# Tiles 5 and 6 of q and k loaded four tokens to a partition, W_in in six pieces, and a new order for all engines

## The chip, the core and the metric

The kernel runs on one core of a Trainium2 chip. The time is device time in microseconds (us) of one execution; a kernel's time is the median of several. Matrix products run on TensorE (PE, with its weight loads as PEld), elementwise work on VectorE (DVE) and ScalarE (ACT). GpSimd (POOL) issues most loads and stores, SyncE (SP) the transposing DMAs. Each engine works through its own instructions in program order and waits for the others by semaphores.

## The reference

```python
scores = scale * q @ k.T + bias          # per batch (4) and head (8); 768 tokens, head dimension 64
keep = is_global | is_local              # first 8 keys, and the 96 latest up to the token itself
a = softmax(where(keep, scores, -1e9))
x = (a @ v).transpose(0, 2, 1, 3).reshape(3072, 512)
h = x @ w_in                             # 512 -> 2048
out = (h - tanh(h)) @ w_out              # 2048 -> 512
```

The bias is ALiBi: minus a slope per head times the distance (96 for a far global key). All inputs and the output are float32.

## The kernel before

The 3072 tokens are 24 tiles of 128. They are worked in an order of "turns" u = 0 to 23: the first tile of each of the four batches (turns 0 to 3), then the other tiles, five per batch. "Tile 5" in what follows is turn 5. Below, a dot and a number after a letter names one piece of work; these are the words of the string `ORDER`.

- **Loads.** `lq.u`, `lk.u`, `lv.u` load q, k, v of a tile; `in.j` a piece of W_in, `out.j` a quarter of W_out. For turns 0 to 2 (`u < HW`) q and k come as float32 on ACT's and SP's queues and are cast by `cq.u` and `ck.u` (a trailing `/a` or `/d` says whether ACT or DVE does it). All other loads are POOL's and cast to bfloat16 on the way. For `u < ROWS` `load_rows` puts four tokens of a head into one partition, so that each piece read is 4 x 64 floats (1 KB); from `ROWS` on, and for v, `load_natural` puts one token into one partition, in pieces of 64 floats (256 B).
- **Transposes.** `T.u` turns q and k so that the head dimension lies on the partitions. Up to turn 6 (`u < PE_T`) PE does it. In natural form it is 8 matmuls of 128 columns against `ident` (L313). In the four-token form it is, for turns 3 and up, 16 matmuls with 64-column weights against the permuted identity `turn` (L322), and for turns 0 to 2 it is 8 with 128 columns (L318). `Te.u.1` (k) and `Te.u.0` (q) copy the result from PSUM to `qk`, in the four-token form with a permutation. From turn 7 on, SP issues DMA transposes (L334), from `kq` to `qk`.
- **Attention.** `S` scores (L353; from turn 11 on three blocks at a time), `E` exp on ACT, `M` times the mask table on DVE, `AV` (L379), `R` reciprocal and scaling on DVE. `X.u` and `Xe.u` transpose the result into `xT` (by PE up to turn 7, later by SP's DMAs). `bm.m` and `em.m` build the three mask tables; `K` and `V` copy the global keys and values.
- **MLP.** Tiles are taken in groups: turns 0 and 1 alone, then pairs, then fours. `m1.g.f` is h for 512 output columns of group g (L421): 16 matmuls of 128 columns for a single tile, 8 of 256 for a pair, 4 of 512 for a four. `th` is tanh on ACT (L431), `g` the difference on DVE (L437). `m2.u.0.a` (L446) is a quarter of the sum for the output of tile u: 4 matmuls of 512 columns. `ev` copies it out of PSUM, `st` stores it.
- **Pieces of W_in.** `in_end = [2, 4, 8, 12, 16]`: `in.0` and `in.1` hold two blocks of 128 columns each (512 KB of float32), `in.2` to `in.4` four each (1 MB). `m1.0.0` and `m1.1.0` need `in.0` and `in.1`; `m1.2.0` needs `in.0`, `m1.2.2` needs `in.1`; `m1.0.4`, `m1.1.4`, `m1.2.4` and `m1.2.6` need blocks 4 to 7.
- **Order.** `ORDER` is one list of all pieces of work; each engine takes those that are its own, in that order. `zero:b` is a matmul on zeros whose result nobody uses; it keeps PE at work. `HOMES` gives the buffers and PSUM banks. In the trace of this kernel POOL issues a load only once the load eight places before it has landed, as soon as that many are under way.

What a tile's transpose in PE is, in the code:

```python
if u >= ROWS:
    for p in range(NP):
        nc.tensor.transpose(t[:, p * P : (p + 1) * P], s[:, j, p * P : (p + 1) * P], ident)
...
for hh in range(2):
    c = (hh * R4 + r) * Dh
    nc.tensor.matmul(o[hh * Dh : (hh + 1) * Dh], s[:, j, c : c + Dh], turn, start=True, stop=True)
```

Of the kernel before, what the change touches and what calls it, by code (L numbers as in the profile page):

```python
# [27 lines left out]
Te.6.1/d Te.6.0/a g.2.14 X.4 m2.2.0.1 Xe.4/a lq.9 m2.0.0.2 lv.7 S.6 m2.2.0.2 E.6.1 K.6 m2.1.0.2 E.6.0 M.6.1 m2.3.0.1
M.6.0 m2.2.0.3 T.7 AV.6 ev.2.0/a X.5 R.6 m2.0.0.3 Xe.5/a T.8 m2.3.0.2 V.6 ev.0.0/a T.10 m1.3.12 m1.3.0 th.3.12 T.9
m2.1.0.3 g.3.12 th.3.0 m1.3.8 g.3.0 ev.1.0/a S.7 st.1.0 th.3.8 lq.18 X.6 E.7.1 K.7 m2.3.0.3 g.3.8 lv.12 Xe.6/d m1.3.10  # L30
E.7.0 ev.3.0/d lq.14 m1.3.2 M.7.1 th.3.10 lv.9 m1.3.4 M.7.0 th.3.2 lv.10 g.3.10 S.8 th.3.4 g.3.2 m1.3.6 lq.12 E.8.1
g.3.4 m1.3.14 lk.11 th.3.6 M.8.1 AV.7 lq.11 E.8.0 g.3.6 m2.4.0.0 lk.13 R.7 th.3.14 m2.4.0.1 lk.12 M.8.0 S.9 V.7 lk.14
m2.4.0.2 g.3.14 E.9.0 st.0.0 K.9 X.7 m2.4.0.3 E.9.1 M.9.0 lv.11 S.10 Xe.7/d T.11 lq.13 ev.4.0/a M.9.1 AV.8 E.10.0
m1.4.8 K.10 R.8 T.12 E.10.1 m1.4.10 M.10.0 m2.5.0.0 th.4.8 M.10.1 Xe.8 th.4.10 AV.9 g.4.8 m1.4.2 T.14 V.9 g.4.10
m1.4.6 th.4.2 R.9 m1.4.0 lq.23 th.4.6 g.4.2 Xe.9 AV.10 th.4.0 g.4.6 m2.5.0.1 lk.16 T.13 R.10 m2.5.0.2 g.4.0 Xe.10
m1.4.4 V.10 S.11 th.4.4 lq.22 m2.5.0.3 g.4.4 E.11.1 K.12 m2.6.0.0 K.11 ev.5.0/d E.11.0 m1.4.14 M.11.1 st.5.0 E.12.0
st.2.0 M.11.0 m1.4.12 lv.13 th.4.14 M.12.0 AV.11 lq.15 th.4.12 m2.7.0.0 g.4.14 lk.15 g.4.12 m2.6.0.1 R.11 lk.18
m2.7.0.1 V.11 Xe.11 lq.16 S.12 lv.18 m2.6.0.2 E.13.0 m2.7.0.2 lv.19 E.13.1 M.13.0 m1.5.8 T.15 E.12.1 M.13.1 m1.5.2
th.5.8 M.12.1 m2.7.0.3 T.18 th.5.2 g.5.8 m1.5.4 ev.7.0/a g.5.2 T.16 AV.12 th.5.4 m1.5.0 R.12 m1.5.12 th.5.0 V.12 Xe.12
g.5.4 m1.5.10 th.5.12 lk.19 g.5.0 AV.13 g.5.12 th.5.10 lv.14 m2.6.0.3 R.13 st.4.0 m1.6.2 ev.6.0/a lv.15 g.5.10 Xe.13  # L40
m1.5.6 th.6.2 lk.21 m1.6.12 g.6.2 th.5.6 lq.17 S.13 g.5.6 th.6.12 st.6.0 m1.6.4 g.6.12 lk.17 E.14.1 K.15 K.14 m1.5.14
lq.19 E.15.0 M.14.1 m2.8.0.0 lv.16 th.5.14 M.15.0 m2.8.0.1 E.14.0 g.5.14 m2.8.0.2 th.6.4 M.14.0 m1.6.6 g.6.4 m2.8.0.3
th.6.6 AV.14 g.6.6 ev.8.0/a m1.6.0 T.17 R.14 m1.6.10 th.6.0 V.14 Xe.14 S.14 g.6.0 th.6.10 T.19 m2.10.0.0 g.6.10 E.15.1
K.16 m2.9.0.0 lq.20 E.16.1 M.15.1 m2.10.0.1 st.3.0 E.16.0 M.16.1 lv.17 m2.9.0.1 M.16.0 AV.15 lk.22 m1.6.8 R.15 m1.6.14
th.6.8 V.15 Xe.15 m2.9.0.2 g.6.8 th.6.14 AV.16 g.6.14 m2.9.0.3 V.16 R.16 m2.10.0.2 ev.9.0/a Xe.16 S.15 st.9.0 lq.21
m2.10.0.3 T.22 E.17.0 K.17 m2.11.0.0 ev.10.0/d E.17.1 m2.11.0.1 M.17.0 E.18.0 M.17.1 m1.7.6 M.18.0 S.16 th.7.6
m2.11.0.2 g.7.6 E.18.1 K.19 T.21 m1.7.10 E.19.0 M.18.1 m2.11.0.3 th.7.10 M.19.0 m1.7.1 ev.11.0/a g.7.10 m1.7.2 st.11.0
th.7.1 st.8.0 m1.7.12 g.7.1 th.7.2 lk.20 m1.7.15 g.7.2 th.7.12 st.10.0 m1.7.13 g.7.12 lv.20 th.7.15 m1.7.0 g.7.15
lv.21 th.7.13 AV.17 g.7.13 lv.23 th.7.0 m1.7.3 R.17 E.19.1 lk.23 m1.7.11 V.17 Xe.17 th.7.3 M.19.1 AV.18 th.7.11 g.7.0
m1.7.7 T.20 R.18 m1.7.4 th.7.7 g.7.11 Xe.18 m1.7.9 th.7.4 g.7.7 m1.7.5 th.7.9 g.7.4 m1.7.8 g.7.9 th.7.5 T.23 m1.7.14  # L50
g.7.3 th.7.8 g.7.5 AV.19 th.7.14 m2.13.0.0 g.7.8 V.19 m2.13.0.1 R.19 m2.13.0.2 g.7.14 Xe.19 S.17 m2.12.0.0 E.21.0 K.21
K.20 m2.13.0.3 E.20.0 M.21.0 m2.12.0.1 ev.13.0/d E.20.1 m2.12.0.2 M.20.0 st.13.0 lv.22 M.20.1 S.18 m1.8.2 E.22.1 K.22
# [537 lines left out]
```

## Time and profile before

| | |
|---|---|
| median of 3 runs | 213.57 us (213.45 to 213.74) |
| the profiled execution: time | 213.46 us |
| the profiled execution: span of its instructions | 211.2 us |
| granted TensorE clock | 1.00 in every window of the trace |
| busy share: PE, PEld, DVE, ACT, POOL | 97%, 58%, 63%, 57%, 36% |
| last matmul ends | 208.07 us after the start of the span |

All later times are us from the start of the span. The time of an execution is 2.26 us more than its span; a change of the span is taken to be a change of the time. The views used are the page's sums, the waits by engine (who waited for whom), the chain of work that ended last, the timelines by engine (start, duration, engine, line, operation, destination and source, count, and in brackets the idle time before it and what ended it), and for a DMA its time from issue to landing.

When the loads that POOL issues first landed, from these answers:

| load | lk.3 | lq.3 | lv.1 | lv.0 | lv.2 | in.1 | in.0 | lv.3 | in.2 | lk.5 | in.3 | lk.4 | lq.4 | lq.5 | in.4 | lq.7 | out.0 |
|---|---|---|---|---|---|---|---|---|---|---|---|---|---|---|---|---|---|
| landed | 6.60 | 9.21 | 10.42 | 11.26 | 12.09 | 13.41 | 14.79 | 15.63 | 18.66 | 19.50 | 22.05 | 22.72 | 23.40 | 24.26 | 26.89 | 27.63 | 30.18 |

### The profile page before, as it was taken

Reading aid. Unit: us, or ns where it says so; the run is one execution under the profiler, and the core shown is the slowest. Engines: PE = TensorE matmul, PEld = TensorE weight load, DVE = VectorE, ACT = ScalarE, POOL = GpSimd, SP = SyncE. Lnnn points to the kernel's source line nnn. Section 1 sums busy time; section 2 is a strip of 40 time slices with the busy share of each in tenths; the row PEclk is TensorE's granted clock in tenths of the full one; section 3 lists DMA queues with packets and bytes.
Section 4 is the critical chain, followed back from the end, with each engine's and each line's share of the span. In section 5 each row is a group of like instructions: output and inputs, shape, how many; then the busy total and the mean of one; then the engine's idle time right before and its main releaser. Section 6 shows DMA issues by size and latency. Waiting matters only on the chain.

```text
span 211.2 us, 4631 instructions
## 1 busy us (share of the span) xinstructions
PE 204.8 (97%) x1867; PEld 122.8 (58%) x1867; DVE 132.8 (63%) x269; ACT 120.1 (57%) x177; POOL 77.0 (36%) x101
## 2 busy tenths in 40 slices
...
DMA packets 100885, 27.55 MB, mean 130 GB/s; under 512 B 91841, under 2 KB 99265, under 8 KB 100865
## 3 DMA queue, kind: packets, MB, share of 16 engines
...
q1 hardware_dynamic: 28048, 8.13, 22.4%
...
q8 instruction: 14, 0.23, 0.4%
q14 instruction: 7, 0.05, 0.1%
...
## 4 chain that ended last, share of the span: by engine, by line
PE 90%; DMA 5%; POOL 3%; issue 0%; ACT 0%; POOLq 0%
PE ps L446 40%; PE ps L421 39%; PE ps L353 5%; DMA w_in_bf<-in_moe_w_in_dram 5%; PE ps L379 5%; POOL vb L298 2%; POOL kq L295 1%; POOL w_in_bf L301 1%; PE ps L399 0%; PE ps L313 0%; PE ps L322 0%; POOL rel L236 0%; ACT ot L230 0%; POOLq L236 0%; POOLq L571 0%
## 5 line engine op out<-in xcount | busy, mean ns | idle before, releaser
L421 PE MATMUL ps<-xT,w_in_bf 128*128 128x256 bf16 (+2 forms) x640 | 90.6, 294 | 1.1 <-DMA w_in_bf<-in_moe_w_in_dram 1.1
L446 PE MATMUL ps<-w_out_bf,g 128*128 128x512 bf16 (+2 forms) x400 | 90.2, 371 | 0.0
L437 DVE TENSOR_TENSOR g<-ps,th 128x512 bf16<-128x512 f32 x96 | 65.0, 687 | 37.8 <-ACT th L431 36.5
L431 ACT ACTIVATE th<-ps 128x512 f32<-128x512 f32 x96 | 57.3, 598 | 50.5 <-PE ps L421 49.9
L421 PEld LDWEIGHTS <-w_in_bf 128*128 128x128 bf16 x640 | 56.2, 98 | 28.8 <-DMA w_in_bf<-in_moe_w_in_dram 1.5
L446 PEld LDWEIGHTS <-g 128*128 128x128 bf16 x400 | 37.0, 98 | 39.0
L360 ACT ACTIVATE pr<-ps 128x1024 bf16<-128x1024 f32 x44 | 42.9, 1025 | 12.7 <-PE ps L353 12.0
L455 POOL DMA_DIRECT2D out_dram<-ot x21 | 11.9, 571 | 93.9 <-ACT ot L230 76.5
L364 DVE TENSOR_TENSOR pr<-pr,mk 128x1024 bf16<-128x1024 bf16 x44 | 29.5, 686 | 7.8 <-ACT pr L360 7.5
L298 POOL DMA_DIRECT2D kq<-in_q_dram x19 | 17.2, 907 | 17.5 <-DMA qk<-kq 14.7
L230 ACT COPY ot<-ps 128x512 f32<-128x512 f32 (+2 forms) x20 | 11.3, 564 | 20.7 <-PE ps L446 17.9
L298 POOL DMA_DIRECT2D vb<-in_v_dram x24 | 21.8, 919 | 2.3 <-DMA w_in_bf<-in_moe_w_in_dram 1.7
L298 POOL DMA_DIRECT2D kq<-in_k_dram x19 | 17.3, 923 | 11.3 <-DMA qk<-kq 6.0
L388 DVE TENSOR_TENSOR x<-ps,rden 128x512 bf16<-128x512 f32 x24 | 16.6, 691 | 0.8
L379 PEld LDWEIGHTS <-pr 128*128 128x128 bf16 x352 | 13.5, 97 | 4.3 <-DVE pr L364 0.7
L379 PE MATMUL ps<-vb,pr 128*128 128x65 bf16 x352 | 14.7, 193 | 0.5 <-DVE pr L364 0.5
L353 PEld LDWEIGHTS <-qk 64*128 64x128 bf16 x352 | 10.1, 94 | 5.7 <-issue 4.4
L353 PE MATMUL ps<-qk 64*128 64x128 bf16 x192 | 9.5, 218 | 0.1
L353 PE MATMUL ps<-qk,qk 64*128 64x128 bf16 x160 | 7.8, 217 | 0.0
L387 DVE RECIPROCAL rden<-ps 128x8 f32<-128x8 f32 x24 | 4.8, 199 | 4.1 <-PE ps L379 3.9
L232 DVE COPY qk<-qk 128x32 bf16<-128x32 bf16 x16 | 3.5, 254 | 6.0 <-PE ps L353 6.0
L232 DVE COPY vb<-vb 8x512 bf16<-8x512 bf16 x16 | 6.0, 374 | 1.5 <-PE ps L379 1.5
...
## 6 DMA issues: line engine op xcount, KB each, us to landing
...
```

The source lines that it names most:

```text
L230: nc.scalar.copy(out=out, in_=in_)
L298: eng(e).dma_start(out=dst, in_=rows_of(src, u).rearrange("h p d -> p h d"))
L353: nc.tensor.matmul(bank(("s", u, o), hh)[:, p * P : (p + 1) * P], buf(("qk", back[u] if o else u))[r, 1, p, :], buf(("qk", u))[r, 0, p, :] ...
L360: nc.scalar.activation(d, banks(("s", u, o), 0, 1), AF.Exp, bias=0.0, scale=scale)
L364: nc.vector.tensor_tensor(out=t, in0=t, in1=mk[:, mask_of(u, o)], op=ALU.mult)
L379: nc.tensor.matmul(t[:, h // (H // 2), h % (H // 2), :], buf(("p", u, o))[:, slot(h), :], buf(("v", back[u] if o else u))[:, h, 0 : Dh + 1 ...
L388: nc.vector.tensor_tensor(out=buf(("x", u)).rearrange("q (a h) d -> q a h d", a=2), in0=t[:, :, :, 0:Dh], in1=rden.to_broadcast([P, 2, H / ...
L421: nc.tensor.matmul(t[:, (f - f0) * n : (f - f0 + 1) * n], w_in_bf[j][:, c, fo : fo + P], x[:, c, 0:n], start=(c == 0), stop=(c == CD - 1),)
L431: nc.scalar.activation(h_view(buf(("th", g, f0)), g, m), h_view(bank(("h", g, f0)), g, m), AF.Tanh, bias=0.0, scale=1.0)
L437: nc.vector.tensor_tensor(out=buf(("g", g))[:, f0 : f0 + m, 0:n], in0=h_view(bank(("h", g, f0)), g, m), in1=h_view(buf(("th", g, f0)), g, ...
L446: nc.tensor.matmul(bank(part)[:, 0 : c1 - c0], buf(("g", g))[:, f, t * P : (t + 1) * P], w_out_bf[f // FJ][:, f % FJ, c0:c1], start=(f == ...
L455: eng(e).dma_start(out=out[turn_of[u] * P : (turn_of[u] + 1) * P, c0:c1], in_=buf(("ot", u))[:, c0:c1])
```

## The change

`ROWS` goes from 5 to 7: q and k of turns 5 and 6 come four tokens to a partition, and their `T` and `Te` take the form that goes with it. The third piece of W_in (blocks 4 to 7) becomes two of 512 KB, so that blocks 8 to 11 are now `in.4` and 12 to 15 `in.5`. `ORDER` and `HOMES` are written anew from end to end; below is the new order up to the scores of tile 7, and the old one up to the same place. The work behind it is the same in kind and number, in another order. The loop in `m1` only spells its steps another way. Zero matmuls go from 13 to 11.

```diff
-    ROWS = 5
+    ROWS = 7
...
-    in_end = [2, 4, 8, 12, 16]
+    in_end = [2, 4, 6, 8, 12, 16]
...
-        for f in range(0, CF, m):
+        for f, m in [(f, m) for f in range(0, CF, m)]:
...
-lq.1 lk.1 zero rel ones.0 zero:7 dist lk.3 lq.0 lk.0 zero:7 zero:7 turn lq.2 lk.2 lq.3 slopes zero:7 table zero:7 lv.1
-first bm.1 ident ones.1 lv.0 bm.0 em.1 lv.2 cq.1/d zero:7 ck.1/d em.0 zero:7 in.1 T.1 in.0 cq.0/a zero:7 ck.0/d lv.3
-zero:7 Te.1.1/d Te.1.0/a zero:3 T.0 in.2 S.1 Te.0.1/a Te.0.0/d zero:6 E.1.0 cq.2/d S.0 zero:7 ck.2/d zero:7 lk.5 E.0.0
-M.1.0 T.2 T.3 Te.2.1/d Te.2.0/a in.3 AV.1 M.0.0 Te.3.1/a S.2 lk.4 Te.3.0/a R.1 AV.0 E.2.0 S.3 lq.4 R.0 bm.2 E.3.0 X.1
-M.2.0 lq.5 Xe.1/d em.2 AV.2 X.0 M.3.0 in.4 m1.1.0 Xe.0/a R.2 lq.7 AV.3 th.1.0 R.3 X.2 m1.0.0 Xe.2/a g.1.0 X.3 th.0.0
-Xe.3/d out.0 m1.0.4 g.0.0 lv.5 m1.2.0 th.0.4 m1.2.4 g.0.4 th.2.0 m1.2.2 g.2.0 th.2.4 lv.4 m1.2.6 g.2.4 th.2.2 out.1
-m1.1.4 g.2.2 th.2.6 lv.6 g.2.6 T.4 th.1.4 m1.1.8 lq.6 Te.4.0/d Te.4.1/a g.1.4 m1.0.8 th.1.8 g.1.8 S.4 th.0.8 lk.8
-m1.2.8 E.4.1 K.4 g.0.8 lk.6 m1.2.12 th.2.8 M.4.1 T.5 E.4.0 g.2.8 m1.1.12 Te.5.1/d Te.5.0/a m1.0.12 M.4.0 out.2 th.2.12
...
+lq.1 lk.1 zero rel ones.0 zero:7 dist lk.3 lq.0 lk.0 zero:7 zero:7 lq.2 lk.2 lq.3 turn zero:7 first table zero:7 lv.1
+ident slopes zero:7 zero:7 lv.0 ones.1 bm.2 cq.1/a lv.3 ck.1/d bm.0 em.2 lv.2 T.1 em.0 in.1 cq.0/d zero:7 ck.0/a in.0
+zero:7 Te.1.0/d zero:3 Te.1.1/a T.0 zero:3 in.2 S.1 Te.0.1/a Te.0.0/d E.1.0 ck.2/d S.0 cq.2/d in.3 E.0.0 M.1.0 T.2 T.3
+Te.2.1/a Te.2.0/d in.4 AV.1 Te.3.0/a M.0.0 S.2 lk.5 Te.3.1/a R.1 AV.0 E.2.0 S.3 lk.4 R.0 bm.1 E.3.0 X.1 lq.5 M.2.0
+Xe.1/a M.3.0 AV.2 em.1 X.0 lq.4 R.2 AV.3 Xe.0/a R.3 X.2 in.5 m1.0.0 Xe.2/a X.3 th.0.0 m1.1.0 Xe.3/d out.0 g.0.0 m1.2.0
+th.1.0 lk.6 g.1.0 m1.2.2 th.2.0 g.2.0 m1.0.4 th.2.2 g.2.2 m1.1.4 th.0.4 out.1 g.0.4 m1.2.4 th.1.4 lv.4 g.1.4 m1.2.6
+th.2.4 lq.10 g.2.4 m1.0.8 th.2.6 lq.6 g.2.6 T.5 th.0.8 lv.5 m1.1.8 Te.5.0/d Te.5.1/a g.0.8 T.4 th.1.8 m1.2.10 Te.4.1/d
+Te.4.0/a lk.9 g.1.8 m1.0.12 th.2.10 g.2.10 S.4 th.0.12 m1.2.12 g.0.12 E.4.0 out.2 K.4 m1.2.14 E.4.1 M.4.0 lk.7 S.5
+th.2.12 M.4.1 m1.2.8 th.2.14 g.2.12 E.5.0 m2.3.0.0 g.2.14 out.3 th.2.8 K.5 M.5.0 m2.1.0.0 E.5.1 lv.6 g.2.8 m2.2.0.0
+lv.7 M.5.1 AV.4 m2.0.0.0 lq.8 V.4 R.4 m2.3.0.1 lq.7 T.6 lk.8 AV.5 Te.6.1/d Te.6.0/a m2.2.0.1 R.5 lq.9 m2.0.0.1 V.5
+lk.10 m2.0.0.2 X.4 m2.1.0.1 Xe.4/a S.6 m2.3.0.2 E.6.1 K.6 m2.0.0.3 E.6.0 M.6.1 X.5 ev.0.0/d m2.1.0.2 Xe.5/a M.6.0
+m1.1.12 T.7 m1.3.0 th.1.12 T.8 g.1.12 m2.2.0.2 th.3.0 g.3.0 AV.6 T.9 m1.3.14 R.6 m2.2.0.3 V.6 th.3.14 T.10 g.3.14
+m2.1.0.3 ev.2.0/a S.7 ev.1.0/a m1.3.4 st.1.0 E.7.1 K.7 lv.8 m2.3.0.3 th.3.4 M.7.1 E.7.0 lq.14 m1.3.2 g.3.4 ev.3.0/d
...
```

More of the change, by code (lines that the diff above doesn't have):

```diff
@@ L28 @@
[L28 to L52, printed above, removed]
@@ new lines @@
+th.5.10 m1.6.10 R.13 T.16 m1.6.8 g.5.10 th.6.10 g.6.10 m2.7.0.3 Xe.13 th.6.8 g.6.8 m1.6.0 ev.7.0/a lk.19 T.18 m1.5.6
+th.6.0 st.3.0 g.6.0 m1.5.0 lk.17 th.5.6 g.5.6 m2.6.0.3 lv.22 th.5.0 g.5.0 S.13 lv.16 ev.6.0/a m2.8.0.0 lq.17 K.14
+E.15.0 K.15 m1.6.14 lv.15 E.14.0 M.15.0 m1.6.2 lq.19 th.6.14 M.14.0 E.14.1 m1.6.4 g.6.14 lv.18 th.6.2 m2.8.0.1 M.14.1
+lk.22 th.6.4 g.6.2 m2.8.0.2 lq.20 g.6.4 m2.8.0.3 st.6.0 T.17 st.4.0 m1.6.6 ev.8.0/a S.14 th.6.6 T.19 g.6.6 m2.9.0.0
+E.15.1 K.16 m2.10.0.0 E.16.0 M.15.1 T.22 AV.14 M.16.0 m2.9.0.1 E.16.1 R.14 m2.9.0.2 M.16.1 Xe.14 m1.6.12 V.14
@@ new lines @@
+Xe.18 m1.7.12 th.7.5 R.19 m1.7.1 th.7.12 V.19 Xe.19 g.7.5 m1.7.4 th.7.1 g.7.12 g.7.1 m1.7.15 th.7.4 g.7.4 m1.7.14
+th.7.15 g.7.15 m1.7.8 th.7.14 g.7.14 m2.13.0.0 th.7.8 g.7.8 m2.13.0.1 S.17 m2.12.0.0 K.20 E.21.0 K.21 m2.13.0.2 E.20.1
+M.21.0 m2.12.0.1 E.20.0 M.20.1 m2.13.0.3 M.20.0 S.18 ev.13.0/a st.13.0 m2.12.0.2 E.22.0 K.22 lv.21 m1.8.11 E.22.1
+M.22.0 AV.20 th.8.11 M.22.1 m2.12.0.3 E.21.1 R.20 m1.8.6 ev.12.0/a M.21.1 Xe.20 S.19 st.12.0 th.8.6 g.8.11 m1.8.0
+E.23.0 g.8.6 V.20 m1.8.1 th.8.0 M.23.0 AV.21 g.8.0 th.8.1 m2.15.0.0 E.23.1 V.21 g.8.1 AV.22 R.21 m1.8.8 M.23.1 Xe.21
@@ new lines @@
+m1.8.7 th.8.8 V.22 R.22 m1.8.13 th.8.7 g.8.8 Xe.22 AV.23 g.8.7 th.8.13 m1.8.3 R.23 m1.8.14 th.8.3 g.8.13 Xe.23
+m2.15.0.1 g.8.3 th.8.14 g.8.14 m1.8.12 m1.8.15 th.8.12 g.8.12 m1.8.5 th.8.15 g.8.15 m1.9.2 th.8.5 g.8.5 m1.9.3 th.9.2
+g.9.2 m1.9.7 th.9.3 g.9.3 m1.9.0 th.9.7 g.9.7 m1.8.10 th.9.0 g.9.0 m1.8.2 th.8.10 g.8.10 m1.9.9 th.8.2 g.8.2 m1.8.4
+th.9.9 g.9.9 m1.9.14 th.8.4 g.8.4 m2.18.0.0 th.9.14 g.9.14 m1.9.11 m2.18.0.1 th.9.11 g.9.11 m2.14.0.0 m1.9.1 m1.9.12
+th.9.1 g.9.1 m2.19.0.0 th.9.12 g.9.12 m1.9.5 m2.16.0.0 th.9.5 g.9.5 m2.19.0.1 m2.17.0.0 m1.8.9 m2.17.0.1 th.8.9 g.8.9
@@ new lines @@
+m1.9.10 m2.14.0.1 th.9.10 g.9.10 m1.9.4 m2.14.0.2 th.9.4 g.9.4 m1.9.8 m2.16.0.1 th.9.8 g.9.8 m2.17.0.2 m2.20.0.0
+m2.18.0.2 m1.9.6 m2.19.0.2 th.9.6 g.9.6 m2.19.0.3 m2.17.0.3 ev.19.0/a st.19.0 m2.21.0.0 ev.17.0/a st.17.0 m2.14.0.3
+m2.15.0.2 ev.14.0/a m1.9.15 st.14.0 m2.16.0.2 th.9.15 g.9.15 m2.16.0.3 m2.18.0.3 ev.16.0/a st.16.0 m2.22.0.0 ev.18.0/a
+st.18.0 m2.15.0.3 st.7.0 m1.9.13 ev.15.0/a m2.21.0.1 th.9.13 st.15.0 m2.22.0.1 g.9.13 m2.22.0.2 m2.21.0.2 m2.20.0.1
+m2.21.0.3 m2.22.0.3 ev.21.0/a st.21.0 m2.20.0.2 ev.22.0/a st.22.0 m2.20.0.3 m2.23.0.0 ev.20.0/a st.20.0 st.8.0
@@ L66 @@
+m2.23.384.0 ev.23.0/a st.23.0 ev.23.384/a st.23.384
 """
@@ new lines @@
+p.0.0:1 av.0:6,7 x.0:1 xt.0:3 xT.0:1 tr.1.0:6 tr.1.1:4 qk.1:0 s.1.0:0,1 p.1.0:0 av.1:0,1 x.1:0 xt.1:2 xT.1:0 tr.2.0:6
+tr.2.1:7 qk.2:2 s.2.0:2,3 p.2.0:2 av.2:6,7 x.2:2 xt.2:2 xT.2:2 tr.3.0:4 tr.3.1:5 qk.3:3 s.3.0:4,5 p.3.0:3 av.3:4,5
+x.3:0 xt.3:2 tr.4.0:7 tr.4.1:2 qk.4:5 s.4.0:0,1 s.4.1:2,3 p.4.0:4 p.4.1:0 av.4:4,5 x.4:1 xt.4:0 xT.3:3 tr.5.0:0
+tr.5.1:1 qk.5:4 s.5.0:4,5 s.5.1:0,1 p.5.0:1 p.5.1:2 av.5:4,5 x.5:2 xt.5:0 tr.6.0:0 tr.6.1:1 qk.6:6 s.6.0:4,5 s.6.1:0,1
+p.6.0:0 p.6.1:3 av.6:4,5 x.6:0 xt.6:5 xT.4:1 qk.7:7 s.7.0:4,5 s.7.1:0,1 p.7.0:1 p.7.1:4 av.7:4,5 x.7:1 xt.7:4 qk.8:8
@@ new lines @@
+s.8.0:6,7 s.8.1:0,1 p.8.0:0 p.8.1:2 av.8:4,5 x.8:2 xT.5:2 qk.9:9 s.9.0:4,5 s.9.1:0,1 p.9.0:3 p.9.1:1 av.9:2,3 x.9:1
+qk.10:10 s.10.0:6,7 s.10.1:4,5 p.10.0:0 p.10.1:4 av.10:6,7 x.10:0 xT.6:0 qk.11:4 p.11.0:1 p.11.1:2 av.11:2,3 x.11:2
+qk.12:5 s.11.0:2,3 s.11.1:6,7 s.12.0:4,5 p.12.0:3 p.12.1:0 av.12:2,3 x.12:1 xT.7:3 qk.13:6 s.12.1:4,5 s.13.0:6,7
+s.13.1:2,3 p.13.0:1 p.13.1:4 av.13:2,3 x.13:0 qk.14:1 p.14.0:0 p.14.1:3 av.14:2,3 x.14:2 qk.15:7 s.14.0:2,3 s.14.1:4,5
+s.15.0:6,7 p.15.0:2 p.15.1:1 av.15:6,7 x.15:1 qk.16:8 s.15.1:2,3 s.16.0:4,5 s.16.1:6,7 p.16.0:4 p.16.1:0 av.16:2,3
@@ new lines @@
+th.1.4:1 h.1.8:6 th.1.8:1 h.1.12:2 th.1.12:3 h.2.0:1 th.2.0:2 g.2:2 h.2.2:6 th.2.2:3 h.2.4:5 th.2.4:2 h.2.6:2 th.2.6:3
+h.2.8:2 th.2.8:2 h.2.10:4 th.2.10:2 h.2.12:7 th.2.12:0 h.2.14:6 th.2.14:1 h.3.0:1 th.3.0:0 g.3:0 h.3.2:6 th.3.2:3
+h.3.4:2 th.3.4:2 h.3.6:0 th.3.6:1 h.3.8:1 th.3.8:2 h.3.10:2 th.3.10:3 h.3.12:7 th.3.12:0 h.3.14:0 th.3.14:1 h.4.0:4
+th.4.0:3 g.4:1 h.4.2:3 th.4.2:1 h.4.4:0 th.4.4:2 h.4.6:2 th.4.6:0 h.4.8:0 th.4.8:1 h.4.10:5 th.4.10:0 h.4.12:7
+th.4.12:3 h.4.14:6 th.4.14:2 h.5.0:1 th.5.0:2 g.5:2 h.5.2:6 th.5.2:2 h.5.4:7 th.5.4:3 h.5.6:7 th.5.6:1 h.5.8:4
```

86 lines of the change are left out of this document (35 added, 51 removed).

## The prediction

> **What bounds it.** I read the page's sums first, then the waits by engine, the chain that ended last, and the timelines of PE, DVE, ACT and POOL up to 32 us. PE is busy for 97% of the span, and the chain is PE's for 90% of it:
>
> ```profile
> PE 204.8 (97%) x1867; PEld 122.8 (58%) x1867; DVE 132.8 (63%) x269; ACT 120.1 (57%) x177; POOL 77.0 (36%) x101
> ...
> PE 90%; DMA 5%; POOL 3%; issue 0%; ACT 0%; POOLq 0%
> ```
>
> The rest of the chain lies at its start (start, duration, what):
>
> ```profile
> 8.20 10.46 DMA w_in_bf<-in_moe_w_in_dram
> 18.66 0.05 issue
> 18.70 5.45 PE ps L421 x64
> ```
>
> The third piece of W_in (8.20 to 18.66) releases PE at 18.70. From there on PE never waits again: the waits give it one wait of weight,
>
> ```profile
> PE ps L421 <- DMA w_in_bf<-in_moe_w_in_dram: 1.1, 1, 1.1
> ```
>
> and the work left at 18.70, 189.4 us by the rows, ends at 18.70 + 189.4 = 208.1, where PE does end. So two things count: when the unbroken stream of PE work begins and how much of it is left then, and what the stream costs. DVE, ACT and DMA have slack behind 18.70, as long as they do not come late.
>
> **The added PE work.** Tiles 5 and 6 turn from 8 matmuls each into 16 with 64-column weights. Both forms are in the trace (tile 4 has 16, tile 5 has 8):
>
> ```profile
> 17.17 0.40 PE L399 MATMUL ps<-ident,x 128*128 128x128 bf16 x4
> 18.70 5.45 PE L421 MATMUL ps<-xT,w_in_bf 128*128 128x128 bf16 x64 [1.13 <-DMA w_in_bf<-in_moe_w_in_dram]
> 24.09 0.64 PE L322 MATMUL ps<-turn,kq 128*64 128x128 bf16 x16
> 24.66 1.96 PE L421 MATMUL ps<-xT,w_in_bf 128*128 128x128 bf16 x32
> ...
> 28.86 0.61 PE L313 MATMUL ps<-ident,kq 128*128 128x128 bf16 x8
> 29.31 1.89 PE L421 MATMUL ps<-xT,w_in_bf 128*128 128x128 bf16 x31
> ```
>
> Start to next start the 16 take 24.66 - 24.09 = 0.57 us and the 8 take 29.31 - 28.86 = 0.45. The 16 cost a little more ahead of themselves: the 64 matmuls from 18.70 are two m1 of a single tile (0.90 each: the 32 from 24.66 hold two, and the second starts at 25.56) and four of a pair (0.87), 5.28 in all, and end at 23.98, yet T.4 starts at 24.09. Such a 0.1 stands ahead of the half-array scores too (24.66 + 1.80 = 26.46, S.4 at 26.55) and not ahead of T.5 (27.10 + 2 x 0.87 = 28.84, T.5 at 28.86). So one tile costs 0.12 to 0.22 more; I take 0.22, as both rows show it, and **+0.44 us** for two. Nothing hides it: it stands in the stream.
>
> Their copies Te, on DVE, take 0.69 instead of 0.41 (T.4 and T.5 in the trace); on ACT 0.58 either way. That is 0.28 more per tile on an engine that is 63% busy, and S.5 and S.6 come over 4 us of PE work behind their T. Nothing, unless DVE falls behind.
>
> **The loads.** Four loads change form. Loads land one behind the other: lk.4 and lq.4 (four tokens) 0.67 and 0.68 us after the load before, lk.5 and lq.5 (natural) 0.84 and 0.87. So four save some 0.7 us of DMA time, from 19 us on, where PE waits for no load: worth nothing. Splitting the third piece: in.0, 512 KB, landed 1.38 behind in.1, so two take 2.76 where 1 MB took 3.03 (in.2) or 2.55 (in.3): -0.3 to +0.2, taken as +0.2. It lies on the way only if m1.0.4 waits for it, which is worked out next. The new order also puts lv.3 ahead of in.1 and in.0. The same eight loads then stand up to in.0 as stood before up to lv.3, so in.0 lands at about 15.63 instead of 14.79, and in.2 and in.3 by 18.66 + 0.2 = 18.9.
>
> **The new start.** PE now has m1.0.0, X.3, m1.1.0, m1.2.0 and m1.2.2 to do before the first block of the split piece, where before only two m1 were ahead of it. So in.3 at 18.9 stops being what is late, and the question is when m1.0.0 starts. It needs in.0 (15.63), X.2 behind it in PE's order, and Xe.0. X.2 needs R.2, at the end of a run of DVE work that in the old trace goes without a gap from the cast of tile 2:
>
> ```profile
> 9.64 0.43 DVE L232 CAST kq<-f 128x512 bf16<-128x512 f32 x1 [0.18 <-DMA f<-in_k_dram]
> 9.99 0.69 DVE L364 TENSOR_TENSOR pr<-pr,mk 128x1024 bf16<-128x1024 bf16 x1
> ...
> 14.07 0.42 DVE L232 COPY xT<-ps 128x512 bf16<-128x512 bf16 x1
> 14.40 0.68 DVE L364 TENSOR_TENSOR pr<-pr,mk 128x1024 bf16<-128x1024 bf16 x1
> 15.00 0.20 DVE L387 RECIPROCAL rden<-ps 128x8 f32<-128x8 f32 x1
> ```
>
> lk.2 lands at 9.62 either way. Now ck.2 goes first and cq.2 behind it, which puts M.1.0 a cast (0.35 start to start) later, at 10.34; and Xe.1 (0.33) leaves this run for ACT. By the same start-to-start steps (0.60 for M, Te, M; 0.84 for each R; 0.60 for M.2.0 and M.3.0) R.2 starts at 10.34 + 4.68 = 15.02, against 15.00. X.2 then starts at 16.0 (15.99 before) and takes 0.23: not before 16.23. ACT's run: ck.0 (landing 7.28) is now ACT's, 0.62 instead of DVE's 0.43, then Te.1.1; T.0 moves from 7.79 to 7.98, a zero matmul stands behind it, and S.1 moves from 8.38 to about 8.75, so E.1.0 from 8.82 to 9.19. From there, by ACT's starts in the old trace (0.92 for an E, 0.48 for a Te, 0.90 for em), E.0.0, three Te, E.2.0 and E.3.0, Xe.1 (0.5) and em.1 come before Xe.0, which then runs from 15.7 to 16.3. So m1.0.0 starts between 16.23 and, if T.2 waits for both casts (0.2), 16.5; I take **16.35**.
>
> **The sum.** From m1.0.0 on PE has the old 189.4, plus m1.0.0 to X.3 (0.95), X.3 (0.23) and m1.1.0 (0.90), which were done by 18.70 before, and 0.44 for the transposes: 191.9. (m1.2.0 and m1.2.2 stood behind 18.70 before and are in the 189.4.) 16.35 + 191.9 = 208.25, against 208.1: +0.15. Without the 0.44 it would be -0.3: what the shorter wait gives, the two transposes take back. The tail behind PE's end is the same (one copy, one store on SP). The profiled execution took 213.46, 0.11 under the median of the runs; I add 0.15 to the median: **213.7 us**. A measurement of this kernel can tell about 0.2% (0.43 us) from no change; 213.14 to 214.0 is no change.
>
> Covers, if the stream starts at 16.35 and loads land as spaced above (1 MB 2.6): in.3 at 18.9 for m1.0.4 at 20.2; in.4 at 21.5 for m1.0.8 at 23.7; lq.5 at 23.5 for T.5 at 24.7; in.5 at 26.8 for m1.0.12 at 27.7. Each is 0.9 or more; a load later than that by x costs x.
>
> **Rivals.** *Tile 7's transposing DMA comes late* (slower, 0.17). lq.7 was the 16th of POOL's loads (landed 27.63); lk.7, landing at 45.45, released T.7, issued on SP at 45.60, landed 50.99; S.7 started at 52.18. Now lq.7 is the 31st, 23 loads behind in.0: 15.63 + 3.0 (in.2, in.3) + 6 x 2.57 (in.4, in.5, four out) + 6 x 0.68 + 9 x 0.84 = 45.7. T.7 then lands between 45.85 + 3.2 (the time of T.23, alone in the queue) = 49.1 and 45.85 + 5.4 = 51.25, and S.7 comes 35.0 us of PE work behind m1.0.0, at 51.35. From 0.1 us beyond the worse end PE waits, and all later PE work with it; on SP T.8 to T.10 queue behind T.7. If POOL's queue runs 0.7 late, about one large load's spread (2.55 to 3.31, out.1): 213.7 + 0.6 = 214.3. For it: the cover falls from 1.2 to 0.1. Against: T.7 landed 1.0 after the last load of that batch (lv.7, 49.95), and the last is now lk.10, at 45.7 + 3 x 0.84 = 48.2.
>
> *ACT's run at the start is later than worked out* (slower, 0.10). ACT's first instruction is now a cast, behind the table load that ended at 4.09. If a cast and an exp each wanted a table, a second load of 1.28 would stand ahead of em.2, ck.0 would move from 7.3 to 8.0 and all behind it by 0.7: 214.4. Against: copies, exp and tanh take turns all through the trace with a single load.
>
> *PE starts with in.0* (faster, 0.07): m1.0.0 at 15.7 gives 207.55, -0.5, so 213.05. DVE's run would have to end 0.6 earlier, while lk.2's landing holds it.
>
> *The fixed cost of a DMA* (slower, 0.03). The three loads from in.1 on landed 1.32, 1.38 and 0.84 apart, so what a load costs by itself lies beside the others. If the added load kept POOL's queue 2 us longer, in.3 would land at 20.9, PE would wait 0.7 there, and lq.7 at 47.7 would bring T.7 up to 1.9 behind S.7: 214.4 to 215.6, say 215.0. The Trainium skill, "DMA: Bandwidth & Descriptors", section "Anatomy of one DMA — SWDGE (gpsimd) path", gives each DMA a fixed 2.0 us, mostly the wait for the write's receipt; as latency that agrees with landings closer than 2 us, as time of the queue it does not.
>
> *The forecast itself* (0.60) covers m1.0.0 from 16.2 to 16.6 and a T of 0.12 to 0.22: 213.4 to 214.0. Another 0.03 is for a stall in the later order, which keeps the same kinds of steps; slower.
>
> That gives faster 0.07, same 0.60, slower 0.33. The range goes from PE starting with in.0 and the cheaper transposes (213.57 - 0.5 - 0.2) to the fixed cost: 212.9 to 215.0.
>
> **What would show it.** Right: no wait of PE on W_in; the first m1 at 16.2 to 16.5, in.3 landed before 20; L322 x64 with 0.57 us per tile; PE gapless to S.7 and beyond; PE's end at 208.2 to 208.3. Wrong: a gap ahead of S.7 or m1.0.12, m1.0.0 at 15.7 or beyond 17, two table loads.

## The result, and the profile after

| | before | after |
|---|---|---|
| median of the first comparison | 213.51 us (4 runs) | 215.19 us (214.74 to 215.32, 3 runs) |
| ratio, 95% interval | | 1.0077 (1.0061 to 1.0093) |
| again, on another chip | 213.53 us (29 runs) | 214.63 us (214.17 to 215.21, 6 runs) |
| ratio, 95% interval | | 1.0051 (1.0037 to 1.0065) |
| the profiled execution: time, span | 213.46, 211.2 us | 215.19, 212.8 us |
| last matmul ends | 208.07 us | 209.63 us |

The change made the kernel slower by 0.5 to 0.8%, and the prediction was 213.7 us (212.9 to 215.0). (A fourth run of the first comparison, 220.1 us at a granted clock of 0.992, is left out; with it the median is 215.25.) In the profiled execution PE's last matmul comes 1.56 us later than before.

The page's sums after, with the chain of work that ended last (share of the span by engine, then by line):

```profile
PE 205.3 (96%) x1881; PEld 122.5 (58%) x1881; DVE 133.3 (63%) x267; ACT 121.6 (57%) x179; POOL 76.8 (36%) x102
...
PE 84%; DMA 8%; DVE 3%; issue 1%; SPq 1%; ACT 1%; POOL 0%; POOLq 0%; DVEq 0%; ACTq 0%
PE ps L446 37%; PE ps L421 37%; PE ps L353 4%; PE ps L379 4%; DMA f<-in_k_dram 3%; DMA out_dram<-ot 3%; DMA qk<-kq 3%; DVE pr L364 1%; DVE x L388 1%; PE ps L322 1%; PE ps L399 1%; SPq L295 1%; DVE kq L232 0%; DVE ot L232 0%; DVE qk L232 0%
```

The sums tell almost nothing: PE's 0.5 us more is about what the longer transposes cost. The chain tells more. Before, it was PE's for 90% and left PE only at the start. Now it is PE's for 84%, and two things are in it that have no business there: a store (`out_dram<-ot`) and a transposing DMA (`qk<-kq`), 3% each. The same chain in order of time (start, duration, what):

```profile
2.43 7.16 DMA f<-in_k_dram
9.61 1.02 DVE kq L232 x2
10.63 0.59 DVE pr L364
...
16.64 0.97 PE ps L421 x16
17.83 7.07 PE ps L421 x96
...
66.29 5.35 DMA qk<-kq
73.06 5.35 DMA out_dram<-ot
78.50 0.70 DVE ot L232
79.25 1.02 PE ps L446 x4
```

The first part is the new start as the prediction had it: the third piece of W_in is gone from the chain, and the load of k of turn 2 (landed 9.59) and DVE's run behind it have taken its place. The last four lines are a path through the middle of the kernel that the prediction did not have. The waits of PE from 16 us on say the same in two lines:

```profile
PE ps L446 <- DVE ot L232: 0.6, 1, 0.6
PE ps L399 <- DVE x L388: 0.4, 1, 0.4
```

The second is X.2 at the start. The first is m2.7.0.0 at 79.25, which waits for the copy of tile 5's output out of the PSUM bank that the two share (bank 1). DVE, PE and POOL around it, from two timelines:

```profile
78.50 0.69 DVE L232 COPY ot<-ps 128x512 f32<-128x512 f32 x1 [1.89 <-DMA out_dram<-ot]
...
79.25 1.02 PE L446 MATMUL ps<-w_out_bf,g 128*128 128x512 bf16 x4 [0.62 <-DVE ot L232]
```

```profile
64.44 1.87 POOL L298 DMA_DIRECT2D kq<-in_k_dram  x2
72.20 0.88 POOL L298 DMA_DIRECT2D kq<-in_q_dram  x1 [5.89 <-DMA qk<-kq]
73.06 0.58 POOL L455 DMA_DIRECT2D out_dram<-ot  x1
```

Read backwards: PE waits for ev.5.0 on DVE. DVE waits 1.89 us for the landing of st.2.0, because ot.2 and ot.5 are one buffer. st.2.0 was copied out by ACT at 51.43, but is issued at 73.06: in POOL's new order it stands behind lq.18. And lq.18 stands still for 5.89 us because it writes the buffer that tile 12's transposing DMA still reads (issued 66.29, landed 71.64). The Trainium skill, "DMA: Bandwidth & Descriptors", section "Anatomy of one DMA — SWDGE (gpsimd) path", says that a DMA's wait for a semaphore is done by the engine that issues it, before it is dispatched. This trace agrees: the waiting load kept a store from being issued that had nothing to do with it. In the old order st.2.0 was issued later still, at 77.14, and no one waited for it: there the buffers went to other users.

Two smaller stalls can't be seen in the waits, because the modelled end of a matmul covers them; they are read from start to start. Four m2 matmuls take 0.87 us, yet m1.7.6 starts 1.18 us after them:

```profile
116.45 0.65 PE L379 MATMUL ps<-vb,pr 128*128 128x65 bf16 x16
116.93 1.03 PE L446 MATMUL ps<-w_out_bf,g 128*128 128x512 bf16 x4
118.11 1.02 PE L421 MATMUL ps<-xT,w_in_bf 128*128 128x512 bf16 x4
```

The 0.31 us is the wait for tile 15's transposing DMA (Xe.15, issued 113.72, landed 118.02). The other stall is in S.9:

```profile
61.10 0.73 DVE L232 COPY xT<-ps 128x512 bf16<-128x512 bf16 x2
...
61.69 0.57 PE L353 MATMUL ps<-qk 64*128 64x128 bf16 x8
62.06 0.42 PE L353 MATMUL ps<-qk,qk 64*128 64x128 bf16 x8
62.42 0.82 PE L446 MATMUL ps<-w_out_bf,g 128*128 128x512 bf16 x3
```

Its 16 matmuls take 0.73 us to the next start, where those of S.5 take 0.56 (31.24 to 31.80): every second one of the first eight writes bank 5, which still holds xt.6 until DVE ends the second of the two copies, Xe.6, at 61.83. So the 1.56 us are: 0.17 in S.9, 0.79 at m2.7.0.0, 0.31 at m1.7.6, and the other 0.29 for the start and the two transposes (forecast 0.15, with m1.0.0 at 16.35 instead of 16.55).

### The profile page after: what moved, and what is told of

The parts are those of the page before. It is cut to its first block, busy times and chain, and to the rows that moved or that the text cites. A ratio compares the mean times of both kernels' runs of the same rounds, so it can differ in the third digit from the quotient of the medians.

```text
span 212.8 us, 4664 instructions
## 1 busy us (share of the span) xinstructions
PE 205.3 (96%) x1881; PEld 122.5 (58%) x1881; DVE 133.3 (63%) x267; ACT 121.6 (57%) x179; POOL 76.8 (36%) x102
## 4 chain that ended last, share of the span: by engine, by line
PE 84%; DMA 8%; DVE 3%; issue 1%; SPq 1%; ACT 1%; POOL 0%; POOLq 0%; DVEq 0%; ACTq 0%
PE ps L446 37%; PE ps L421 37%; PE ps L353 4%; PE ps L379 4%; DMA f<-in_k_dram 3%; DMA out_dram<-ot 3%; DMA qk<-kq 3%; DVE pr L364 1%; DVE x L388 1%; PE ps L322 1%; PE ps L399 1%; SPq L295 1%; DVE kq L232 0%; DVE ot L232 0%; DVE qk L232 0%
## 5 line engine op out<-in xcount | busy, mean ns | idle before, releaser
L364 DVE TENSOR_TENSOR pr<-pr,mk 128x1024 bf16<-128x1024 bf16 x44 | 30.0, 689 | 10.5 <-ACT pr L360 9.7
L230 ACT COPY ot<-ps 128x512 f32<-128x512 f32 (+2 forms) x20 | 11.3, 565 | 19.9 <-PE ps L446 16.2
L298 POOL DMA_DIRECT2D kq<-in_k_dram x17 | 15.5, 925 | 9.6 <-DMA qk<-kq 7.6
L298 POOL DMA_DIRECT2D kq<-in_q_dram x17 | 15.5, 921 | 6.9 <-DMA qk<-kq 5.9
L388 DVE TENSOR_TENSOR x<-ps,rden 128x512 bf16<-128x512 f32 x24 | 16.6, 692 | 0.8
L232 DVE COPY qk<-qk 128x32 bf16<-128x32 bf16 x16 | 4.0, 268 | 6.3 <-PE ps L353 6.3
L230 ACT CAST qk<-ps 128x512 bf16<-128x512 f32 x8 | 4.6, 586 | 3.8 <-PE ps L322 3.8
L232 DVE COPY vb<-vb 8x512 bf16<-8x512 bf16 x16 | 5.3, 332 | 1.4 <-PE ps L379 1.4
```

The source lines that it names most:

```text
L230: nc.scalar.copy(out=out, in_=in_)
L298: eng(e).dma_start(out=dst, in_=rows_of(src, u).rearrange("h p d -> p h d"))
L364: nc.vector.tensor_tensor(out=t, in0=t, in1=mk[:, mask_of(u, o)], op=ALU.mult)
L388: nc.vector.tensor_tensor(out=buf(("x", u)).rearrange("q (a h) d -> q a h d", a=2), in0=t[:, :, :, 0:Dh], in1=rden.to_broadcast([P, 2, H / ...
```

## The experiments

**Is it the store?** Moved in POOL's order, nothing else:

```diff
-... AV.10 lq.18 g.4.0 T.13 m1.4.10 V.10 st.2.0 R.10 ...
+... AV.10 st.2.0 lq.18 g.4.0 T.13 m1.4.10 V.10 R.10 ...
```

> The changed kernel with one word moved: the store of tile 2 (st.2.0) goes ahead of the load lq.18 in POOL's order. Theory (three waits in the new order): in the changed kernel lq.18 held POOL until tile 12's transposing DMA had read its buffer (72.20), so st.2.0 was issued at 73.06 and landed at 78.41, ev.5.0 on DVE waited for that (78.50) and PE's m2.7.0.0 for ev.5.0 (79.25 instead of 78.46). With the store issued at about 66.3 this wait of 0.79 us goes: 215.25 - 0.79 = 214.45 us, with PE gapless from S.9 to tile 15. Rival (the gain is given back): PE comes earlier to the next late thing, Xe.15 or a load, and waits there: 215.0 to 215.3. Rival (DVE itself is late, ev.5.0 behind the masks): no change, 215.25, and ev.5.0 still starts at 78.5.

Measured: 213.74 us (12 runs; before 213.51), ratio 1.0012 (0.9998 to 1.0027). POOL, DVE and PE of this kernel, from three timelines:

```profile
66.50 0.71 POOL L455 DMA_DIRECT2D out_dram<-ot  x1
72.73 0.89 POOL L298 DMA_DIRECT2D kq<-in_q_dram  x1 [5.52 <-DMA qk<-kq]
```

```profile
77.26 0.69 DVE L232 COPY ot<-ps 128x512 f32<-128x512 f32 x1 [0.30 <-PE ps L446]
```

```profile
77.06 1.91 PE L421 MATMUL ps<-xT,w_in_bf 128*128 128x256 bf16 x16
78.81 1.03 PE L446 MATMUL ps<-w_out_bf,g 128*128 128x512 bf16 x3
```

The load still waits 5.52 us, but the store is out, DVE waits only for PE, and PE goes on without a bracket. The stall at m2.7.0.0 is gone. The time came out 0.7 us under the 214.45 expected: it fell by 1.45 us against the first measurement of the change, and by 0.9 against the second (214.63, another chip). Part of the first is outside the traced span: the median span of the change is 212.9 us and then 212.6, that of this kernel 211.9, so the span fell by 1.0 and 0.7, about the 0.8 of the stall.

**All three places, and what a cover is worth.** Besides the store, m2.4.0.2 goes ahead of S.9, and m2.11.0.2 ahead of m1.7.6, so that PE has work while it would wait. That is the first of three kernels; the second has the same order and also takes `ROWS` back to 5 (natural loads). The third is the kernel before with `ROWS = 7` alone.

```diff
-... S.9 lq.12 m2.4.0.2
+... m2.4.0.2 S.9 lq.12
-... st.10.0 m1.7.6 lv.17 M.18.0 Xe.16 S.16 ... g.7.6 m2.11.0.2 E.19.1
+... st.10.0 m2.11.0.2 m1.7.6 lv.17 M.18.0 Xe.16 S.16 ... g.7.6 E.19.1
-    ROWS = 7          (the second kernel only; the third the other way round)
+    ROWS = 5
```

> The same, and two more words moved: m2.11.0.2 goes ahead of m1.7.6, which waited 0.30 us for the transposing DMA of tile 15; m2.4.0.2 goes ahead of S.9, whose second half waited 0.17 us for the copy of xt.6 out of its bank. Three waits: 215.25 - 0.79 - 0.30 - 0.17 = 214.0 us, that is the kernel before (213.5) plus the start and the transposes of tiles 5 and 6 (0.30 by the two traces) and what is left. Given back: over 214.6.

> As the one before, and ROWS back to 5: tiles 5 and 6 of q and k load one token to a partition again and turn in 8 matmuls of 128 columns. If the two transposes stand in PE's stream with 0.22 us each, 0.44 less: 213.55 us. If half-width weights cost nothing ahead of themselves, 0.24 less: 213.75. If the four loads in pieces of 256 B come too late for this order (0.16 us of DMA each, 0.65 together), PE waits at one of T.5, m1.0.12 or S.7, and nothing is won: 214.0 or more.

> The kernel before with ROWS = 7 alone: order and W_in pieces as they were. Transposes in the stream: 213.51 + 0.44 = 213.95 us (0.24 if the weights ahead cost nothing: 213.75). Rival, the lighter loads pay for them: 213.5 or less, with loads behind 19 us landing 0.65 earlier and PE still without a wait there.

Measured: 215.85 us (5 runs), 1.0113 (1.0098 to 1.0127); 214.32 us (11 runs), 1.0035 (1.0009 to 1.006); 214.67 us (7 runs), 1.0055 (1.0033 to 1.0078). All three times missed the forecast. (The second lies at the figure of the rival, late loads, but PE waits at none of the places that the rival named.) The first shows why a cover can't just be moved:

```profile
117.93 1.03 PE L421 MATMUL ps<-xT,w_in_bf 128*128 128x512 bf16 x4
118.89 0.40 PE L353 MATMUL ps<-qk,qk 64*128 64x128 bf16 x8
119.12 0.39 PE L353 MATMUL ps<-qk 64*128 64x128 bf16 x8
119.34 0.39 PE L353 MATMUL ps<-qk,qk 64*128 64x128 bf16 x8
120.36 1.89 PE L421 MATMUL ps<-xT,w_in_bf 128*128 128x512 bf16 x8 [0.63 <-DVE g L437]
```

m1.7.6 no longer waits ahead of itself, but m1.7.3 waits 0.69 us: it uses bank 0 as m1.7.6 does, must wait for tanh and difference of m1.7.6, and m2.11.0.2 had been the work between. 0.31 was taken away and 0.69 put in. The kernel with natural loads shows what the transposes cost: m1.0.0 to S.6 takes 25.41 us instead of 25.87, 0.46 for two tiles.

**The stalls mended without a new one, and the change itself once more.** As above, but m2.11.0.3 moves up into the place that m2.11.0.2 leaves; the last kernel again has `ROWS = 5`. The changed kernel itself ran on the same chip.

```diff
-... g.7.6 E.19.1 lk.21 K.19 m1.7.3 ... lq.21 m2.11.0.3 g.7.3
+... g.7.6 m2.11.0.3 E.19.1 lk.21 K.19 m1.7.3 ... lq.21 g.7.3
```

> The changed kernel as it is, on the same chip and against the same runs of the kernel before as the next three. Theory (the three stalls in the later order, 0.79 + 0.31 + 0.20 us, beside the 0.30 us of the forecast, make up the 1.56 us by which the last matmul ends later): 215.2. Rival (part of it was the chip of that run: moving the store alone gave back 1.5 us instead of 0.8 in an earlier look on another chip): 214.3 to 214.6.

> The changed kernel with the three places mended without robbing another: st.2.0 ahead of lq.18, m2.4.0.2 ahead of S.9, m2.11.0.2 ahead of m1.7.6 and m2.11.0.3 in its old place (bank 0 still gets a cover of one m2 between m1.7.6 and m1.7.3). Theory: 215.2 - 0.79 - 0.31 - 0.20 = 213.9 if counted from the profile of the changed kernel, 213.74 - 0.19 - 0.35 = 213.2 if counted from the run with the store moved; the trace shows no stall behind TensorE's steady start but the two transposes' 0.44 us. Rival (a stall taken away only shows the next one): 213.7 or more, with a wait of 0.3 us or more at another place of the order.

> The kernel of the run before last in this list with the three stalls mended, and tiles 5 and 6 loaded one token to a partition as in the kernel before (16 transposing matmuls fewer a tile). Theory (the transposes of four tokens to a partition cost 0.22 us a tile in TensorE's stream and nothing hides it): 0.45 us under the run with the stalls mended, so 212.7 to 213.4. Rival (the loads of 128-byte pieces land later and bring a stall that the four-token form avoided): the same time as with the stalls mended, with a wait at T.5 or T.6.

Measured: 214.63 us (6 runs), 1.0051 (1.0037 to 1.0065); 214.28 us (12 runs), 1.0033 (1.0015 to 1.0052); 213.53 us (12 runs), 1.0014 (0.9986 to 1.0042). As times these say little: each of these kernels and those of the last two steps spreads by 1 to 2.7 us from run to run (the kernel before by 1.0 to 1.9), the changed kernel itself came out at the rival's figure, the other two lie above their forecasts, and mending two more stalls looks like nothing against moving the store alone. The traces say more. With the three mended, PE's waits from 16 us on are

```profile
PE ps L446 <- issue: 0.6, 4, 0.2
PE ps L399 <- DVE x L388: 0.4, 1, 0.4
```

No engine holds it up any more (the four of 0.2 stand where matmul records are missing, and are made up a few matmuls later; one real 0.22 is left ahead of m1.7.0). The profiled executions of the new order, with the start of m1.0.0 and PE's stretch from there to its last matmul (the last row is from an experiment further down; the one that delays ck.2 is left out):

| kernel | lk.2 lands | m1.0.0 | last matmul | m1.0.0 to last |
|---|---|---|---|---|
| the change | 9.59 | 16.55 | 209.63 | 193.08 |
| the change again | 9.70 | 17.47 | 210.18 | 192.71 |
| store moved | 9.90 | 16.90 | 209.26 | 192.36 |
| three moved | 9.73 | 16.77 | 209.28 | 192.51 |
| three moved, natural loads | 10.11 | 17.83 | 209.88 | 192.05 |
| stalls mended | 9.32 | 16.33 | 208.37 | 192.04 |
| stalls mended, natural loads | 9.90 | 16.90 | 208.48 | 191.58 |
| stalls mended, third piece of W_in whole | 10.11 | 17.77 | 209.81 | 192.04 |

So the time has two parts. The stretch is fixed by the order: 193.08 falls to 192.04 as the stalls go (in the second execution of the change the stall at m1.7.6 did not come), and to 191.58 with 16 matmuls fewer per tile. The start is not: it varied by 1.5 us, and most of it follows lk.2. In five of the eight m1.0.0 comes 6.96 to 7.04 us after its landing. In the change again it is 7.77, and lk.0 had been late as well: it landed at 8.39 instead of 7.0 to 7.8. In the two others (7.72 with three moved and natural loads, 7.66 in the last row) the granted clock, in tenths over 40 slices of the span, has a dip that the other six don't have:

```profile
PEclk9969999999999999999999999999999999999999
```

It is half the full clock for 3.4 us, from 10.7 to 14.1 us and from 11.7 to 15.1, in the middle of PE's part of the start. In the last row the loads of turn 0 were on time (lk.0 7.05, lq.0 6.57), so the dip is what is left for its 0.7 us; with three moved and natural loads lq.0 was late too (7.65 instead of 6.5 to 6.9), and no run separates the two.

**Does the old order hide that spread?** Both orders get the same delay: ck.2 is made three times.

```diff
-... zero:7 ck.2/d zero:7 lk.5          (the kernel before)
+... zero:7 ck.2/d ck.2/d ck.2/d zero:7 lk.5
-... ck.2/d S.0 cq.2/d                  (stalls mended)
+... ck.2/d ck.2/d ck.2/d S.0 cq.2/d
```

> The kernel before with ck.2 (VectorE's copy of k of turn 2 to bfloat16) made three times instead of once: about 0.75 us more of VectorE behind the landing of lk.2, on the way to everything that turn 2 and the runs behind it need. Theory (in the old order the gapless stretch starts when the third piece of W_in lands at 18.66 us, 1.1 us after X.3; a start that is late by less is hidden): 213.5 to 213.7, m1.0.4 still near 18.7 us. Rival (every delay of the start is paid): 214.2.

> The changed kernel with the three stalls mended, and ck.2 made three times, as in the run before this one: the same 0.75 us in the same place. Theory (in the new order nothing stands between the turn-2 data and TensorE's gapless stretch, so m1.0.0 starts 7.0 us behind the landing of lk.2 plus what is added): m1.0.0 7.7 us behind that landing, and 0.7 us above the run with the three stalls mended, 214.2 to 215.0. Rival (the start's spread was something else on those chips): m1.0.0 still 7.0 us behind the landing and the time unchanged, 213.5 to 214.3.

Measured: 213.95 us (12 runs), 1.0025 (1.0005 to 1.0045), and 215.27 us (6 runs), 1.0094 (1.0065 to 1.0123). The first lies between the forecast (213.7 at most) and the rival's 214.2, the second 0.3 above its range; the delay itself came out larger than the 0.75 us reckoned with. DVE in the new order, first with the stalls mended, then with the delay:

```profile
9.35 1.06 DVE L232 CAST kq<-f 128x512 bf16<-128x512 f32 x2 [0.27 <-DMA f<-in_k_dram]
10.33 0.67 DVE L364 TENSOR_TENSOR pr<-pr,mk 128x1024 bf16<-128x1024 bf16 x1
```

```profile
9.87 2.01 DVE L232 CAST kq<-f 128x512 bf16<-128x512 f32 x4 [0.61 <-DMA f<-in_k_dram]
11.80 0.67 DVE L364 TENSOR_TENSOR pr<-pr,mk 128x1024 bf16<-128x1024 bf16 x1
```

M.1.0 comes 1.93 instead of 0.98 us after the first cast: 0.95 more; the load itself landed 0.52 later in this execution. Together 1.47, and m1.0.0 moved from 16.33 to 17.80 (1.47), the last matmul from 208.37 to 209.84 (1.47). All of it is paid. In the kernel before with its delay, lk.2 landed 0.80 later and M.1.0 came another 1.25 later, 2.05 in all; m1.0.0 moved from 16.22 to 18.28 (2.06), but the gapless stretch only from 18.70 to 19.39:

```profile
18.28 1.06 PE L421 MATMUL ps<-xT,w_in_bf 128*128 128x128 bf16 x16
19.17 0.39 PE L399 MATMUL ps<-ident,x 128*128 128x128 bf16 x4
19.39 2.80 PE L421 MATMUL ps<-xT,w_in_bf 128*128 128x128 bf16 x32
```

There is no bracket ahead of m1.0.4 any more: the wait for W_in, 1.3 us from start to start, is used up, and of the 2.06 us only 0.69 is paid. (In this execution the piece itself landed at 19.20, so the late chain cost at most 0.2 beyond it; over all runs the delay cost the old order 0.44 us by the medians, the new one 1.0, though there the two medians are from two chips, and three of the six delayed runs have a mean clock of 0.992.) So that wait was also a cushion. The new order took it away, and an execution in which lk.2 lands late now pays for it in full.

**The split of the W_in piece, taken out of the new order and put alone into the old one:**

```diff
-in_end = [2, 4, 6, 8, 12, 16]          (stalls mended)
+in_end = [2, 4, 8, 12, 16]
...
-in_end = [2, 4, 8, 12, 16]             (the kernel before)
+in_end = [2, 4, 6, 8, 12, 16]
```

> The changed kernel with the three stalls mended, but the third piece of W_in as one load again (f 4 to 7 together, as in the kernel before); the order of TensorE is untouched. Theory (in this order m1.0.0, m1.1.0, m1.2.0 and m1.2.2 stand ahead of m1.0.4, the first matmul that reads f 4 to 7, which is due near 21 us, so the piece may land at 18.7 and the split buys nothing): the same time as with the split, 213.4 to 213.9, no wait on W_in. Rival (the split is what lets TensorE run on from 16.5 us): a wait on W_in ahead of m1.0.4 and 0.5 us or more lost.

> The kernel before with only the split of the third piece of W_in (two loads, four DMAs to six numbers, POOL issues one more, about 0.9 us of POOL ahead of lk.5); the order is the old one otherwise. Theory (m1.0.4 reads f 4 to 7, both halves; the second half lands no sooner than the whole piece did, 18.66 us): +0.0 to +0.2, so 213.5 to 213.7, the wait of 1.1 to 1.3 us on W_in ahead of m1.0.4 stays. Rival (the halves land earlier than the whole): 213.0 and a wait of 0.8 us or less.

Measured: 214.13 us (12 runs), 1.0025 (1.0009 to 1.0042), against 1.0033 with the split, so no difference that the intervals show. The stretch from m1.0.0 is 192.04 us again, with in.2 landing whole at 18.86. In the new order four m1 stand ahead of the first use, and the split buys nothing. Alone in the old order: 213.06 us (12 runs), 0.9986 (0.9967 to 1.0005).

```profile
17.71 0.62 PE L421 MATMUL ps<-xT,w_in_bf 128*128 128x128 bf16 x8 [0.46 <-ACT th L431]
19.00 5.01 PE L421 MATMUL ps<-xT,w_in_bf 128*128 128x128 bf16 x56 [0.67 <-DMA w_in_bf<-in_moe_w_in_dram]
```

The first time is 0.2 above its forecast, but PE has no wait on W_in, as forecast. The second, forecast at 213.5 to 213.7, came out as its rival said: 213.0 and a wait on W_in under 0.8 us. In that execution only the first half landed earlier than the whole had (17.66 for 18.66); the second landed at 18.95, and PE did 8 of m1.0.4's 16 matmuls between. That is worth 0.16 us at the last matmul (207.92 for 208.07). The median fell by 0.45, with an interval that still includes no change, and the median span only from 211.3 to 211.2; the rest lies outside what the trace shows (below).

**A version that beats both.** If the start of the gapless stretch sets the end, the old order can start sooner without any new load: m1.2.0 and m1.2.2 need only pieces that have landed.

```diff
-Xe.3/d out.0 m1.0.4 g.0.0 lv.5 m1.2.0 th.0.4 m1.2.4 g.0.4 th.2.0 m1.2.2 g.2.0 ...
+Xe.3/d out.0 g.0.0 lv.5 m1.2.0 m1.2.2 th.2.0 m1.0.4 g.2.0 th.2.2 m1.2.4 g.2.2 th.0.4 ...
```

> The kernel before with its loads and its order kept, but m1.2.0 and m1.2.2 ahead of m1.0.4: they need the first piece of W_in only and xT.2, which is written at 18.04 us, and so can run while m1.0.4 waits for the second piece until 18.70. Theory (the start of TensorE's gapless stretch sets the end one for one): it starts at 18.1 instead of 18.7, so -0.6 us: 212.9. Rival (the 96% busy TensorE finds the time again at a later wait for data that comes no earlier): 213.5, with the 0.6 us in waits behind 20 us.

Measured: 212.98 us (12 runs, before 213.53; 212.9 forecast), ratio 0.9975 (0.9965 to 0.9986); median span 210.8 against 211.3.

```profile
17.72 0.39 PE L399 MATMUL ps<-ident,x 128*128 128x128 bf16 x4
18.63 5.45 PE L421 MATMUL ps<-xT,w_in_bf 128*128 128x256 bf16 x64 [0.52 <-DVE xT L232]
```

The wait on W_in is gone; a shorter one on Xe.3 is left. The profiled execution (213.3 us) was one with a late start, m1.0.0 at 16.83 instead of 16.22, so its stretch starts only 0.07 us sooner and its last matmul ends 0.07 sooner: the gain of 0.55 is in the median, and no trace shows it whole. From S.4 to the last matmul it takes 181.53 us; the kernel before takes 181.52, the split alone 181.52, the delayed copy 181.52. The starts of these four differ by 0.8 us and the time behind S.4 does not: in the old order an earlier start is kept to the end.

## Why the prediction was wrong

- **The new start: right, a little early.** in.0 landed at 15.61 (15.63 forecast), in.3 at 18.86 (18.9), in.5 at 26.98 (26.8), and PE never waited on W_in. M.1.0 came at 10.56 instead of 10.34: the second cast held DVE 0.60 to the next start, not 0.35. From there all steps held: R.2 15.26, X.2 16.24, Xe.0 15.86 to 16.50, m1.0.0 16.55 for 16.35: inside the 16.2 to 16.6 that the forecast covers, just past the 16.5 that it named as a sign of being right.
- **But the start was taken as one number.** Over the eight executions of the table m1.0.0 came between 16.33 and 17.83. The prediction saw that the chain now hangs on lk.2 ("lk.2 lands at 9.62 either way") and did not ask what happens where it lands later. This is part of the slower median and hardly of the profiled difference, where lk.2 landed at 9.59: with the stalls mended the median is still 0.75 us above the kernel before (span 212.0 against 211.3), while the profiled execution, with its early start, is 0.3 us longer in span.
- **The transposes: right.** 0.57 us each, as the rows said; two tiles cost 0.46 by the kernels with natural loads, 0.44 forecast.
- **The stretch: right without its stalls.** 191.9 us were forecast from m1.0.0 on; with the stalls mended it is 192.04, of which 0.22 is the one stall left.
- **The rivals did not come.** T.7 landed at 49.72, 1.9 us ahead of S.7; its DMA took 3.5 us, near the lower of the two durations. (T.23, the source of the lower one, was not alone as the prediction says: Xe.18 landed 1.2 us after T.23 was issued.) There was one table load. The added load cost POOL's queue no 2 us.
- **The step that failed** is the last one: "Another 0.03 is for a stall in the later order, which keeps the same kinds of steps". The list of covers ended at 27.7 us and the walk through the order at S.7. Behind it lay 1.27 us of stalls (0.17, 0.79, 0.31), and moving the store alone brought the median within 0.12% of the kernel before. None of the signs of being wrong that the prediction named lies behind S.7 either. The order behind S.7 was there to be read: st.2.0 behind lq.18, lq.18 on tile 12's buffer, ot.2 and ot.5 in one buffer, o.5.0 and o.7.0 in one bank. That these four meet follows from the names; the size needed POOL's times.
- **The stall at m1.7.6 is a race.** In the change Xe.15 landed at 118.02, and PE, done with the matmuls ahead at 117.80, waited. In the second execution PE came 0.92 us later out of the start and Xe.15 landed only 0.35 later, at 118.37, before m1.7.6 at 118.63: no wait.
- **The clock in single runs.** A stretch of 3.4 us at half clock takes 0.5 x 3.4 / 213 = 0.008 off the mean, so a mean of 0.992 fits one such stretch. Three of the four runs of the three-moved kernel that are longer than its profiled one have 0.992; the fourth (215.85) has full clock, a span of 212.8 and 3.05 us outside the span. For `ROWS = 7` alone in the kernel before, the profiled execution had lk.0 late (9.29) and such a stretch from 9.8 to 13.2. From S.4 to the last matmul it shows 0.46 us (181.98); the five runs at full clock have a median span of 211.8, 0.5 above the kernel before, in line with it. The rest of the 1.16 in the median goes with the clock and with time outside the span.
- **Left open:** what makes the clock fall. A mean under 0.995 stands in 15 of the 80 executions of the new order in all its versions and in 5 of the 80 of the kernel before in the three later comparisons; whether the order has a part in this, no run shows. And why the first float32 loads land when they do.
